# Attention, Mish MLP and gate on one core: eight inner tiles of the second product and the output projection are done by seven-product blocks in a tail, and five of sixteen probability tiles per head are summed by accumulating DMAs

## The chip, the cores and the metric

The kernel is one program on one core of a Trainium2 chip. The time is device time in microseconds (us) of one execution, the median over several. The engines are named as in the profile: PE is TensorE (matmuls; PEld is its weight load), DVE is VectorE, ACT is ScalarE, POOL is GpSimd, SP is SyncE, which here only issues DMAs. Each engine runs its own instructions strictly in the order in which they stand, and waits on semaphores for the others.

## The reference, cut to what matters

```
xn = layernorm(x)                                   # x: 2048 tokens x 1024
q, k, v = split(xn @ wqkv)                          # 32 heads of 32
p = softmax(q @ k.T * 32**-0.5)                     # per head 2048 x 2048
s = (p @ v) @ wo                                    # 1024 -> 1024
h = xn @ w1 + b1                                    # 1024 -> 3584
act = h * tanh(softplus(h))                         # Mish
out = x + s * silu(act @ w2)                        # w2: 3584 -> 1024
```

Everything is float32. Most products are kept accurate by cutting each operand into a high and a low part, and by adding three matmuls (high-high, high-low, low-high).

## The kernel before, in words

The program has four stretches. First, layer norm, the transposed and split activations, and v. Second, q and k by a seven-product block scheme. Third, one long mixed stretch, from about 530 us to the end of the last head, in which five streams share PE: `t` (transposed scores of a key tile, 128 keys x 2048 queries, as four matmuls of 512 columns, L1007), `s` (the same scores the other way round, for the row maxima of the next head, L920), `h` (the first MLP product, 24 matmuls for a tile of 128 inner features x 512 tokens, L1213), `y` (the second MLP product, L1303) and `pv` (probabilities times v, L1054). Fourth, the output projection `op` (L1402), with the silu and the gate behind it (L1495, L1496).

The third stretch is laid out ahead of time: a planner (class `Plan`) with a cost for every operation walks through time and writes each engine's order. Of the operations of an engine that are ready at that moment it takes the one with the lowest key. Operations that belong to the end have the key `2 * total` and are taken when nothing else of that engine is ready. A string of digits (`LEAN`) leans the choice in each piece of 21 us. The order, once written, is fixed; a wait that is longer on the chip than in the plan holds up all that stands behind it on its engine.

Per head there are sixteen key tiles (kt 0 to 15). ACT makes the exponentials of a tile into one of seven buffers `p` (four instructions, L285). PE multiplies the tiles by v in groups of 6, 5 and 5. The sum over keys for the softmax comes from POOL: fifteen additions of 128x2048 tiles into `z` (L1036), in the order of the tiles. When `z` is complete, PE reduces it over partitions (`zp`, L1080); `zp` also ends the life of `z`, of which there is one buffer, so that the first addition of the next head waits for it. ACT and DVE turn `zp` into the reciprocal and scale the head's output (L1091 to L1097).

The MLP makes 4 x 28 tiles of Mish (28 tiles `f` of 128 inner features, 4 chunks of 512 tokens). Each goes through twelve or thirteen instructions of DVE and ACT, ending with the split into high and low (L288, L1269). `y` takes them two at a time: 24 matmuls for each tile, and a DVE addition into the accumulator `yacc` for each block of 128 tokens x 512 columns (L1325). While the last heads run, POOL and DVE split the rows of wo (L296).

## Time and profile before

| what | value |
|---|---|
| median of three runs | 3362.5 us (3362.36 to 3362.78) |
| span of the profiled execution, first to last instruction | 3358.0 us |
| what lies outside the span (median less span; the profile gives no other time of that execution) | 4.5 us |
| PE busy in the span | 3345.8 us |
| POOL, DVE, ACT busy | 2524.7, 2510.8, 2056.5 us |
| granted PE clock | 1.00 in every slice |

A line of the groups reads: source line, engine, operation, output <- inputs, shape, count | busy us, mean ns of one | idle us of the engine just before them, and what ended it. Matmuls overlap in the pipeline, so that the duration of one is longer than the distance to the next; the distance is read from long runs of them.

### The profile page before, as it was taken

What the parts mean: (1) busy time and instruction counts of PE and PEld (TensorE: products, weight loads), DVE (VectorE), ACT (ScalarE), POOL (GpSimd) and SP (SyncE); (2) the same over time, 40 slices, a digit from 0 to 9 for tenths busy, and PEclk for the clock granted to TensorE, in tenths of its full rate; (3) what the DMA queues carried; (4) which work ended last, traced back from release to release, by engine and by line L of the source; (5) the groups of instructions that cost most, each with busy time, mean ns of one, the idle gap of its engine ahead of it and who ended that gap; (6) DMA issues with size and microseconds to landing.
All of it is one profiled execution on the core that took longest, in us unless ns stands there. A gap on an engine that the chain in (4) does not pass through costs nothing.

```text
span 3358.0 us, 45795 instructions
## 1 busy us (share of the span) xinstructions
PE 3345.8 (100%) x16886; PEld 2458.4 (73%) x16886; DVE 2510.8 (75%) x3987; ACT 2056.5 (61%) x3313; POOL 2524.7 (75%) x750
## 2 busy tenths in 40 slices
PE   9999999999999999999999999999999999999999
PEld 7888887776777677776777677777677777767787
DVE  6665678877877778887888688888787888886542
ACT  5233436676766666666676666666667666667621
POOL 1323546999999887888888988888888898889800
PEclk9999999999999999999999999999999999999999
DMA  7865745454565643343335334333344433433482
GB/s 248 298 204 181 242 146 183 140 184 152 169 191 172 221 126 115 105 122 114 101 117 179 111 101 126 101 112 116 101 151 139 116 106 112 130 108 107 140 304 83
DMA packets 291460, 501.56 MB, mean 149 GB/s; under 512 B 88138, under 2 KB 151114, under 8 KB 269130
## 3 DMA queue, kind: packets, MB, share of 16 engines
q1 hardware_dynamic: 271524, 456.95, 43.8%
q10 hardware_dynamic: 19712, 41.69, 3.3%
q8 instruction: 133, 2.18, 0.3%
q14 instruction: 91, 0.75, 0.1%
HBM read 352.55 MB, written 144.97 MB: 148 GB/s over the span
## 4 chain that ended last, share of the span: by engine, by line
PE 96%; DMA 1%; DVE 1%; POOL 1%; issue 0%; ACT 0%; SPq 0%; ACTq 0%; POOLq 0%; DVEq 0%
PE y L1303 18%; PE h L1213 18%; PE t L1007 14%; PE s L920 13%; PE pv L1054 13%; PE op L1402 5%; PE v L354 5%; PE q_y L798 3%; PE q_z L798 2%; PE q_x L798 2%; PE zp L1080 1%; PE s L700 0%; POOL z L1036 0%; PE pt L423 0%; DMA w2r<-in_B_w_dram 0%
## 5 line engine op out<-in xcount | busy, mean ns | idle before, releaser
L1036 POOL TENSOR_TENSOR z<-z,p 128x2048 f32<-128x2048 f32 x448 | 2067.7, 4615 | 98.0 <-ACT p L285 72.9
L285 ACT ACTIVATE p<-t,zero 128x512 f32<-128x512 f32 x2048 | 1377.1, 690 | 560.1 <-PE t L1007 535.7
L926 DVE TENSOR_REDUCE mx<-s 128x1 f32<-128x512 f32 x1984 | 1322.3, 685 | 382.7 <-PE s L920 371.9
L1303 PE MATMUL y<-w,act 128*128 128x512 f32 x2688 | 920.3, 391 | 0.8 <-DVE yacc L1325 0.5
L1007 PE MATMUL t<-qstack,kstack 128*128 128x512 f32 x2048 | 799.1, 393 | 1.1 <-ACT p L285 0.7
L920 PE MATMUL s<-kstack,qstack 128*128 128x512 f32 x1984 | 772.6, 393 | 0.2 <-ACT p L285 0.2
L1213 PE MATMUL h<-xr,w 128*128 128x512 f32 x2016 | 697.7, 391 | 0.4 <-DMA xr<-xs 0.4
L1303 PEld LDWEIGHTS y<-w,act 128*128 128x128 f32 x2688 | 503.3, 188 | 114.3 <-issue 6.7
L1007 PEld LDWEIGHTS t<-qstack,kstack 128*128 128x128 f32 x2048 | 383.8, 188 | 114.8 <-issue 18.0
L1054 PE MATMUL pv<-p,v 128*32 128x512 f32 x4096 | 459.3, 594 | 0.0
L920 PEld LDWEIGHTS s<-kstack,qstack 128*128 128x128 f32 x1984 | 369.6, 188 | 118.5 <-issue 32.1
L1213 PEld LDWEIGHTS h<-xr,w 128*128 128x128 f32 x2016 | 378.3, 188 | 81.2 <-issue 3.4
L1325 DVE TENSOR_TENSOR yacc<-yacc,y 128x512 f32<-128x512 f32 x416 | 282.7, 680 | 82.6 <-PE y L1303 81.5
L1054 PEld LDWEIGHTS pv<-p,v 128*32 128x32 f32 x4096 | 123.3, 110 | 282.7 <-issue 281.1
L1036 POOL TENSOR_TENSOR z<-p,p 128x2048 f32<-128x2048 f32 x32 | 148.1, 4628 | 185.2 <-PE zp L1080 146.6
L1213 PE MATMUL h<-xc,w 128*128 128x512 f32 x672 | 231.3, 391 | 1.3 <-DMA w<-w1s 1.0
L354 PE MATMUL v<-vw,xc 128*128 128x512 f32 x768 | 179.7, 392 | 1.2 <-ACT xc L288 0.7
L354 PEld LDWEIGHTS v<-vw,xc 128*128 128x128 f32 x768 | 142.7, 188 | 32.0 <-ACT xc L288 1.4
L1213 PEld LDWEIGHTS h<-xc,w 128*128 128x128 f32 x672 | 125.9, 188 | 30.5 <-issue 2.5
L288 ACT ACTIVATE act<-h 128x512 fp32r<-128x512 f32 x112 | 66.6, 595 | 88.2 <-DVE h L1262 87.0
L798 PE MATMUL q_y<-xc,wq 128*128 128x512 f32 x480 | 115.3, 389 | 0.0
L798 PEld LDWEIGHTS q_y<-xc,wq 128*128 128x128 f32 x480 | 90.0, 188 | 18.8
(149 smaller groups left out, 2947.4 us busy)
## 6 DMA issues: line engine op xcount, KB each, us to landing
w<-w1s SPq DMA_DIRECT2D x91, 1024.0 KB, 5.4
w<-w2s SPq DMA_DIRECT2D x168, 512.0 KB, 4.0
w2s<-w SPq DMA_DIRECT2D x56, 512.0 KB, 4.0
qstack<-qs SPq DMA_DIRECT2D x96, 256.0 KB, 6.3
kstack<-ks SPq DMA_DIRECT2D x96, 256.0 KB, 5.8
w1s<-w SPq DMA_DIRECT2D x21, 1024.0 KB, 5.8
qs<-qst ACTq DMA_DIRECT2D x32, 512.0 KB, 4.1
ks<-qst ACTq DMA_DIRECT2D x32, 512.0 KB, 3.7
```

The lines of the kernel that those rows point to most:

```text
L285: nc.scalar.activation(out_, in_, fn, bias=zero if bias is None else bias, scale=scale)
L354: nc.tensor.matmul(ps, xc[t // 4][k // HK][:, a, k % HK, (t % 4) * P:(t % 4 + 1) * P], vw[i, k // 2][:, b, k % 2], start=n == 0, stop=n == ...
L798: nc.tensor.matmul(ps, w[:, a, k], xx[:, b, k], start=m == 0 and i in (0, 1, 4), stop=m == 3 * HK - 1, skip_group_check=i not in (0, 1, 4))
L920: nc.tensor.matmul(sp_, qst[h % 3][:, qt * P:(qt + 1) * P], kst[h % 3][:, kc * 512:(kc + 1) * 512], start=True, stop=True)
L926: nc.vector.reduce_max(tiles["mx"][:, qt, kc:kc + 1], tiles[qt, kc], axis=AX.X)
L1007: nc.tensor.matmul(tp, kst[h % 3][:, kt * P:(kt + 1) * P], qst[h % 3][:, c * 512:(c + 1) * 512], start=True, stop=True)
L1036: nc.gpsimd.tensor_tensor(zs[h], pts[T - 1] if kt == 1 else zs[h], pts[T], ALU.add)
L1054: nc.tensor.matmul(pv[h][c * DH:(c + 1) * DH, :], vt[h][:, k, :], pts[T - kt + k][:, c * 512:(c + 1) * 512], start=k == 0, stop=k == NT - 1)
L1213: nc.tensor.matmul(t["h"], w1t[n][:, a, k], xts_[c][k // HK][:, b, k % HK], start=i == 0, stop=i == 3 * KT - 1)
L1303: nc.tensor.matmul(t["y"], acts[n][:, p, s * P:(s + 1) * P], w2t[m_][:, q], start=j == 0 and i == 0, stop=j == YB - 1 and i == 2)
L1325: nc.vector.tensor_tensor(ya, ya, t["y"], ALU.add)
L1402: nc.tensor.matmul(ps[t, dh], ohl[t // 4, k][:, a, s * P:(s + 1) * P], wt[k][:, b, r], start=k == 0 and i == 0, stop=k == KT - 1 and i == 2)
```

## The change

Three things are changed together.

**Deferral.** Of the 28 inner tiles, eight (f = 2, 5, 8, 11, 16, 19, 22, 25) take no part in `y` any more. Their Mish result (`r`, 128 features x 512 tokens, float32) goes to DRAM (`ats`), unsplit. The remaining twenty are taken in ten pairs.

**Tail.** The deferred part is a product of 2048 tokens x 1024 features by 1024 x 1024, the same size as the output projection. Both are done behind the last head as sixteen jobs of 256 tokens: jobs 0 to 7 with the deferred rows of w2 (set `y`), jobs 8 to 15 with wo (set `o`). A job cuts its operands into 2 x 2 blocks (128 tokens x 512 features, and 512 x 512) and forms the four block products from seven products of sums of blocks. Each product is 12 matmuls (4 pieces of 128 x 3 for high and low). The sums of the weight blocks (T1 to T4, in place) and their splits are made once for each set, the sums of the activations (S1 to S4) and their splits for each job. Jobs of set `y` add `ys`, go through silu and are stored (`gs`); jobs of set `o` load that and x and make the output. In the order's rows `yb`, `ob` are the weight blocks of the sets, `yu`, `ou` their split units 0 to 6, `araw` a job's activations, `a3_5` unit 5 of job 3, `op3_x` one of its three accumulators in PSUM, `e3_0` an evacuated copy, `g3` its gate rows.

**Sums in DRAM.** Tiles kt 0, 1, 6, 7 and 11 of each head are no longer added by POOL. kt 0 is written to DRAM (`zd`) by SP; the other four are added there by accumulating DMAs, which POOL issues. Each waits for the one before. After kt 11 SP reads the sum back into a `p` buffer (`zp19` and the like in the order, not to be confused with the PE reduction `zp`), and POOL merges it into `z`. POOL's chain is then ten additions and the merge, where it was fifteen additions; the additions of kt 12 to 15 stand behind the merge.

In the last part of the diff `mm7` is the 12 matmuls of a product, `a_unit` and `b_unit` are a split (ACT the high part, DVE the low part), `after` takes the accumulators out of PSUM, `done` finishes a block, job 7 is `NP - 1`, and `LAG` is three products.

Three constants of the planner go with it (`SLOW`, `Y1`, and 0.5 instead of 4.0 us for `zp` in `LATE_Z`); `LEAN` stays as it was.

```diff
-    SEM, SWITCH, LAND, RATE = 0.07, (0.25, 0.13), 2.0, 0.25e6
+    SEM, SWITCH, LAND, RATE, SUM = 0.07, (0.25, 0.13), 2.0, 0.25e6, 7.0
...
-SLOW, UNTIL = 1.25, 700.0
+SLOW, UNTIL = 1.1, 700.0
+DEFER = (2, 5, 8, 11, 16, 19, 22, 25)
+KEPT = [f for f in range(FT) if f not in DEFER]
+BLOCKS = [KEPT[i:i + 2] for i in range(0, len(KEPT), 2)]
-LEAD, LATE = 5, 4.0
-PS, ACTS, W2S, Y0, Y1 = 7, 3, 5, 0.6, 0.17
+THERE = (0, 1, 6, 7, 11)
+HERE = [kt for kt in range(NT) if kt not in THERE]
+LEAD, LATE, LATE_Z = 5, 4.0, 0.5
+PS, ACTS, W2S, Y0, Y1 = 7, 3, 5, 0.6, 0.25
...
-            op.end = start + took
+            op.end = start + took + (self.SUM if op.bytes else 0.0)
...
     def add(T, pts):
         h, kt = divmod(T, NT)
+        def there(at):
+            if kt:
+                nc.gpsimd.dma_start(zd[h % 2], pts[T], accum_op=ALU.add)
+            else:
+                nc.sync.dma_start(zd[h % 2], pts[T])
+        def back(at):
+            pts[h, "z"] = att.tile([P, S], F32, tag=f"p{at['p']}", name=f"zp{h}")
+            nc.sync.dma_start(pts[h, "z"], zd[h % 2])
+        def merge(at):
+            nc.gpsimd.tensor_tensor(zs[h], zs[h], pts[h, "z"], ALU.add)
...
+        if kt in THERE:
+            d = op("POOL" if kt else "SP", 1.2 if kt else 0.1, need=exps[T] + [dma.get(h)], emit=there, bytes_=P * S * 4,
+                   then=then, key=-1)
+            dma[h] = d
+            if kt == THERE[-1]:
+                dma[h] = op("SP", 0.1, need=[d], emit=back, take=["p"], bytes_=P * S * 4)
+                chain[h] = op("POOL", 4.61, need=[chain[h], dma[h]], emit=merge, give=[("p", dma[h])])
...
-        a = own = op("PE", 1.0, need=[sum_], emit=z_mm, take=["d", "b"], give=["z"], col=True, late=LATE)
+        a = own = op("PE", 1.0, need=[sum_], emit=z_mm, take=["d", "b"], give=["z"], col=True, late=LATE_Z)
...
+        if n % FT in DEFER:
+            o6 = op("DVE", 0.69, need=[o5, o3], emit=d6_, give=[("d", t["own"]), ("b", t["own"]), "h"], kind="mish")
+            put_ops[n] = op("SP", 0.1, need=[o6], emit=put, give=["r"], bytes_=P * 512 * 4)
+            return
...
+    def tail_stream():
+        far = 2 * total
+        def sum_(which, need):
+            return op("POOL", 4.61, need=need, emit=lambda at: b_sum("y", which, nc.gpsimd), key=far)
+        def split(i, need, take):
+            h_ = op("ACT", 1.9, need=need, emit=lambda at: b_high("y", i), take=take)
+            return op("POOL", 4.61, need=[h_], emit=lambda at: b_low("y", i, nc.gpsimd), key=far)
...
+    for j in range(last + 1):
+        for i in range(7):
+            mm7(j, i)
+            nxt = j + 1
+            if j == 0:
+                if i < 6:
+                    a_unit(0, i + 1)
+                if i == 0:
+                    b_low("y", 3, nc.vector)
+                if 0 < i < 4:
+                    b_unit("y", i + 3)
+            later.tick()
+            after(j, i)
+            if j == NP - 1:
+                if i == 3:
+                    b_sum("o", "T4", nc.gpsimd)
+                if i == 4:
+                    b_sum("o", "T1", nc.gpsimd)
+                b_unit("o", i)
+                if i == 0:
+                    b_sum("o", "T2", nc.vector)
+            if nxt <= last:
+                if i == 1:
+                    for which in ("S1", "S2", "S3"):
+                        a_sum(nxt, which, nc.gpsimd, small(f"{nxt}{which}", which))
+                later.at(LAG, lambda nxt=nxt, i=i: a_unit(nxt, i))
+            if i == 1:
+                out_load(j)
+            if i >= 4:
+                for n in {4: (4,), 5: (2, 5), 6: (6,)}[i]:
+                    done(j, n)
```

How the order moves, at three places.

POOL, one head in the middle. Before, fifteen additions in a row (rows of head 17, the middle ones left out):

```order
L1036 TENSOR_TENSOR z17_18797<-p272_18688,p273_18720 128x2048
L1036 TENSOR_TENSOR z17_18797<-z17_18797,p274_18793 128x2048
...
L1036 TENSOR_TENSOR z17_18797<-z17_18797,p286_19358 128x2048
L1036 TENSOR_TENSOR z17_18797<-z17_18797,p287_19404 128x2048
L1036 TENSOR_TENSOR z18_19590<-p288_19451,p289_19488 128x2048
```

Now (head 19, kt 6 is tile p310, kt 11 is p315; `hl` is a 0.2 us subtraction for the next head's maxima):

```order
L1044 DMA zd1_161<-p310_19657 128x2048
L1055 TENSOR_TENSOR z19_19579<-z19_19579,p312_19746 128x2048
L1044 DMA zd1_161<-p311_19707 128x2048
L1055 TENSOR_TENSOR z19_19579<-z19_19579,p313_19783 128x2048
L306 TENSOR_TENSOR hl_3351<-nm20_0_19863,hl_3351 128x16
L1055 TENSOR_TENSOR z19_19579<-z19_19579,p314_19812 128x2048
L1044 DMA zd1_161<-p315_19846 128x2048
L1058 TENSOR_TENSOR z19_19579<-z19_19579,zp19_20031 128x2048
L1055 TENSOR_TENSOR z19_19579<-z19_19579,p316_19925 128x2048
```

The DMA issues stand in POOL's queue between the additions, and the merge stands right behind the last issue, with nothing of POOL's between them.

POOL, the last head. Before, nothing stood between its additions (first, second and last, then the tile of wo that followed):

```order
L1036 TENSOR_TENSOR z31_29501<-p496_29370,p497_29394 128x2048
L1036 TENSOR_TENSOR z31_29501<-z31_29501,p498_29499 128x2048
...
L1036 TENSOR_TENSOR z31_29501<-z31_29501,p511_29984 128x2048
L296 TENSOR_TENSOR wo4_30066<-wr2_30007,wo4_30066 128x1024
```

Now, from its ninth tile on:

```order
L306 TENSOR_TENSOR yu0_0_28693<-yb0_27551,yu0_0_28693 128x2048
L1055 TENSOR_TENSOR z31_28541<-z31_28541,p505_28627 128x2048
L1044 DMA zd1_161<-p507_28752 128x2048
L1055 TENSOR_TENSOR z31_28541<-z31_28541,p506_28672 128x2048
L1399 TENSOR_TENSOR yb0_27551<-yb1_27553,yb0_27551 128x2048
L306 TENSOR_TENSOR yu2l_28708<-yb2_28255,yu2h_28707 128x2048
L1058 TENSOR_TENSOR z31_28541<-z31_28541,zp31_28881 128x2048
L306 TENSOR_TENSOR yu1_1_28917<-yb0_27551,yu1_1_28917 128x2048
L1055 TENSOR_TENSOR z31_28541<-z31_28541,p508_28789 128x2048
L1399 TENSOR_TENSOR yb2_28255<-yb2_28255,yb0_27551 128x2048
L1055 TENSOR_TENSOR z31_28541<-z31_28541,p509_28813 128x2048
...
L1055 TENSOR_TENSOR z31_28541<-z31_28541,p511_28867 128x2048
```

Five passes of the tail's set-up (three splits, two weight sums) stand inside the last head's chain. On PE the reduction of that chain, `zp31`, stands ahead of the tail's first product.

ACT, where the tail goes from set `y` to set `o`. This stretch has no counterpart before.

```order
L298 ACTIVATE ou4_30091<-ob0_29212 128x2048
L298 ACTIVATE a8_2_30107<-araw8_29908 128x512
L298 ACTIVATE ou5_30111<-ob2_29484 128x2048
L295 ACTIVATE g7_30022<-g7_30022,zero_174 128x1024
L298 ACTIVATE a8_3_30130<-araw8_29908 128x512
L298 ACTIVATE ou6_30133<-ob3_29620 128x2048
L295 ACTIVATE g7_30022<-g7_30022,zero_174 128x1024
L298 ACTIVATE a8_4_30152<-8S1_30017 128x512
L298 ACTIVATE e8_0_30155<-op8_x_30139 128x512
```

The copy `e8_0` that frees job 8's first accumulator for its third product stands behind the last units of set `o` and behind both silu instructions of job 7.

More of the change, by code (lines that the diff above doesn't have):

```diff
@@ L990, in p_done @@
         if len(uses[T]) == 2:
-            plan.give("p", max(o.end for o in uses[T]))
+            plan.give("p", max(o.end for o in uses[T]), by=exps[T][0])
     def t_stream():
@@ L1357, in wo_raw @@
-    def wo_raw(name, ks, tile_of, **kw):
-        a = raw_op(name, 2, tile_of, [(("wo", k), wo[k * P:(k + 1) * P, :], []) for k in ks], **kw)
-        for k, o in zip(ks, a):
-            wo_loads[k] = o
-    def wo_op(k, where, eng, **kw):
-        def high(at):
-            wt[k] = where()
-            copy(wt[k][:, 0], raws_["wo", k])
-        def rest(at):
-            low(nc.gpsimd if eng == "POOL" else nc.vector, wt[k][:, 1], raws_["wo", k], wt[k][:, 0])
-        need = kw.pop("need", [])
-        a = op("ACT", 1.05, need=[wo_loads[k]] + need, emit=high, **kw)
-        wo_ops[k] = op(eng, 2.36 if eng == "POOL" else 1.3, need=[a], emit=rest, key=2 * total if eng == "POOL" else None,
-                       both=eng == "DVE")
@@ new lines, in b_low, with a_load @@
+    def b_low(set_, i, eng):
+        low(eng, units[set_, i][1], weights[set_, SOURCE[i]], units[set_, i][0])
+    jobs = [(set_, p) for set_ in "yo" for p in range(NP)]
+    def a_load(j, tile_):
+        set_, p = jobs[j]
+        araw[j] = tile_.rearrange("p (k n) -> p k n", k=KT)
+        if set_ == "y":
+            nc.sync.dma_start(araw[j], ats[p // 2][:, p % 2])
+            return
+        for k in range(KT):
+            nc.sync.dma_start(araw[j][:, k], ot[k][:, p * 256:p * 256 + 256])
@@ new lines, in mm7 @@
+    def mm7(j, i):
+        set_ = jobs[j][0]
+        if i in (0, 1, 4):
+            n = bank_sets[j % 2][KEYS[i]]
+            banks_[j, KEYS[i]] = bank({"b": n}, f"op{j}_{KEYS[i]}")
+        ps = banks_[j, KEYS[i]]
+        m = 0
+        for k in range(HK):
+            for a, b in THREE:
+                nc.tensor.matmul(ps, units[j, i][:, a, k], units[set_, i][b][:, k], start=m == 0 and i in (0, 1, 4),
+                                 stop=m == 3 * HK - 1, skip_group_check=i not in (0, 1, 4))
+                m += 1
@@ new lines, in tt, with after @@
+    def tt(eng, out_, a, b, how):
+        eng.tensor_tensor(out_, a, b, how)
+    def after(j, i):
+        set_, p = jobs[j]
+        ps = banks_[j, KEYS[i]]
+        if i in (0, 1, 3):
+            es[j, i] = tl.tile([P, 512], F32, tag=f"e{i}", name=f"e{j}_{i}", bufs=1 if i == 3 else 2)
+        V, G = nc.vector, nc.gpsimd
+        if i == 0:
+            copy(es[j, 0], ps)
+        elif i in (1, 3):
+            tt(V, es[j, i], ps, es[j, 0], ALU.add)
+        elif i == 4:
+            tt(V, es[j, 3], ps, es[j, 3], ALU.add)
```

356 lines of the change are left out of this document (191 added, 165 removed).

## The prediction

> **What bounds the kernel now.** First the page's head and the busy shares, then the table by stage (us from the start, then busy time and instructions of PE, PEld, DVE, ACT, POOL), then who PE waited for.
>
> ```profile
> span 3358.0 us, 45795 instructions
> PE 3345.8 (100%) x16886; PEld 2458.4 (73%) x16886; DVE 2510.8 (75%) x3987; ACT 2056.5 (61%) x3313; POOL 2524.7 (75%) x750
> PEclk9999999999999999999999999999999999999999
> 700.00:1000.00 300.00, 298.64 (x1535) 214.20 (x1534) 236.73 (x376) 210.85 (x345) 283.46 (x107) 1.00 0.54 170
> 2200.00:2600.00 400.00, 399.59 (x2089) 282.11 (x2088) 319.69 (x509) 273.12 (x434) 348.24 (x82) 1.00 0.41 123
> PE idle L473 <- POOL xc L470: 1.8, 1, 1.8
> PE h L1213 <- DMA w<-w1s: 1.0, 1, 1.0
> ```
>
> PE sets the time in every stage, at full clock, and its longest single wait is 1.8 us, at the start. POOL is next: 94% early, where it also splits weights, 87% later. So a matmul removed is time gained, as long as no wait takes its place. Before, no wait of note exists; the question is how many the new order makes. I sum from the profiled execution: span 3358.0 plus the 4.5 outside it, which is the median, 3362.5.
>
> **Matmuls removed.** By the order `y` falls from 2688 to 1920 and `op` rises from 768 to 2 x 672 = 1344: 192 fewer. Their distance comes from the longest piece of the chain (start, length, what):
>
> ```profile
> 3179.26 174.11 PE op L1402 x768
> ```
>
> 174.11/768 = 0.2267 us, and 192 of them are **-43.5**.
>
> PE leaves the pv/zp form and comes back 114 times where it did 97 times, since zp now goes as soon as it is ready. The price, from one visit (start, length, what):
>
> ```profile
> 2162.66 0.62 PE L1303 MATMUL y<-w,act 128*128 128x512 f32 x2
> 2163.21 5.36 PE L1054 MATMUL pv<-p,v 128*32 128x512 f32 x48
> 2168.50 0.50 PE L920 MATMUL s<-kstack,qstack 128*128 128x512 f32 x1
> 2168.84 0.40 PE L1007 MATMUL t<-qstack,kstack 128*128 128x512 f32 x1
> ```
>
> In: 0.55 - 2 x 0.2267 = 0.10; out: 0.34 - 0.23 = 0.11. 17 visits are **+4**. The same rows give 5.29/6 = 0.88 us for one key tile of pv. The yacc additions and splits that go with `y` lie on DVE and ACT beside PE: nothing.
>
> **POOL against PE, head by head.** The loop that can stall is: zp of a head frees `z`; POOL then does the whole chain of the next head, with everything that stands between; then PE may do that head's zp.
>
> ```profile
> L1036 POOL TENSOR_TENSOR z<-z,p 128x2048 f32<-128x2048 f32 x448 | 2067.7, 4615 | 98.0 <-ACT p L285 72.9
> L1036 POOL TENSOR_TENSOR z<-p,p 128x2048 f32<-128x2048 f32 x32 | 148.1, 4628 | 185.2 <-PE zp L1080 146.6
> L296 POOL TENSOR_TENSOR w<-w2r,w 128x512 fp32r<-128x512 f32 x56 | 72.5, 1295 | 32.6 <-ACT w L288 32.6
> 3100.40 4.62 POOL L1036 TENSOR_TENSOR z<-p,p 128x2048 f32<-128x2048 f32 x1 [5.54 <-PE zp L1080]
> 3105.10 66.82 POOL L1036 TENSOR_TENSOR z<-z,p 128x2048 f32<-128x2048 f32 x14
> ```
>
> Before, POOL waits for zp, not PE for POOL. Counting by the order tests this: from the last-but-one zp to the last, PE has 271 matmuls and 16 tiles of pv (61.4 + 14.1 + about 0.7 = 76.2), POOL 15 additions at 66.82/14 = 4.77 or a little less (70 to 71.5): POOL idles about 5, and the row says 5.54.
>
> Now the same for the change, an addition at 4.67 (4.615 and the gap). Middle heads: ten additions, the merge, four DMA issues: 51.4 + 4 x 1.2 + 0.3 = 56.5 against 65 to 83 of PE. No DMA issue of POOL's stands in the trace. The lower bound is ACT's issue below, 0.34; the upper the addition that it replaces, 4.6; I take 1.2, nearer the issue, since POOL only hands the transfer on.
>
> - **Third head** (560 to 700 us): PE has 204 matmuls and 10 tiles of pv, 55.8. POOL has 51.4, eight splits at 1.3, issues: 67. **+12** (8 to 25). The fifth head, with the wait for DRAM below, adds about **+3**.
> - **Last head**: PE has 182 matmuls and 10 tiles, 50.5. POOL has the 51.4, two sums of weights (9.3), three splits of 128x2048 and three issues (3.6).
>
> ```profile
> L288 ACT ACTIVATE wo<-wr x8: 1042/1053/1062, 3013.1 to 3190.4; 128x1024 fp32r<-128x1024 f32 x8
> L296 POOL TENSOR_TENSOR wo<-wr,wo x4: 2386/2410/2827, 3016.6 to 3181.0; 128x1024 fp32r<-128x1024 f32 x4
> L296 DVE TENSOR_TENSOR wo<-wr,wo x4: 1212/1225/1662, 3160.7 to 3191.5; 128x1024 fp32r<-128x1024 f32 x4
> ```
>
> A split of 128x2048 is thus 4.8 on POOL: three are 14.5, and POOL's total is 78.8. PE stands at zp31 for **+28** (25 to 38), with y and pv all done and the tail queued behind it.
>
> **The sums in DRAM.** After the kt 11 exponentials come the issue, the accumulation A, the read-back B, the merge and four additions, then zp.
>
> ```profile
> w<-w1s SPq DMA_DIRECT2D x91, 1024.0 KB, 5.4
> w1s<-w SPq DMA_DIRECT2D x21, 1024.0 KB, 5.8
> xr<-xs SPq DMA_DIRECT2D x12, 1024.0 KB, 7.8
> 3333.09 0.34 ACTq L1500 DMA_DIRECT2D out_dram<-x  x1
> DMA packets 291460, 501.56 MB, mean 149 GB/s; under 512 B 88138, under 2 KB 151114, under 8 KB 269130
> ```
>
> B is 5.4 to 7.8. A is not in the trace: at least a plain write, 5.8, at most read and write in turn, 11.2; I take 7.5, nearer the write, since a stream can overlap both. A + B = 13.3. By the order PE has 40.6 of work between the end of kt 11's scores and zp in the tightest middle heads. Off go 0.9 for the exponential and the hops, 1.2 for the issue, and 24.6 for the merge, four additions and the next head's first issue; 14.0 is left for A + B, and 16 in the median head: **0**. At A + B = 19 (the upper ends) the shortfalls over the heads add up to 77. POOL itself stands still during A + B, but has that slack. The `p` buffers don't tie up more: the five tiles wait for their pv group anyway.
>
> **The tail.** A job is 84 matmuls, 19.0; a product 2.72. In an ordinary job DVE has about 10 to 12 and POOL 10 to 14: covered. Two jobs are not, because their weight splits are made as they go, through chains that cross three engines. Further rows:
>
> ```profile
> L296 DVE TENSOR_TENSOR wq<-raw,wq 128x512 fp32r<-128x512 f32 x20 | 15.5, 778 | 6.5 <-ACT wq L288 6.4
> L1496 DVE TENSOR_TENSOR x<-x,y 128x512 f32<-128x512 f32 x32 | 22.1, 692 | 1.1
> L288 ACT ACTIVATE wq<-raw 128x512 fp32r<-128x512 f32 x29 | 17.9, 623 | 30.1 <-PE q_x L798 13.8 <-PE q_z L798 10.5 <-issue 3.9
> L285 ACT ACTIVATE rz<-rz,zero 128x512 f32<-128x512 f32 x32 | 23.5, 733 | 0.3
> L1094 DVE SCALAR_TENSOR_TENSOR zp<-zp,rz 128x512 f32<-128x512 f32 x32 | 22.1, 692 | 0.1
> L285 ACT ACTIVATE y<-y,zero 128x1024 f32<-128x1024 f32 x16 | 18.3, 1142 | 31.3 <-DVE x L1496 31.2
> ```
>
> From the wo rows a 128x2048 high is about 1.9 on ACT, and a low 2.4 to 3.3 on DVE; I take 2.6.
>
> - **Job 0** (us from zp). DVE's normalisation of the last head stands ahead of S1 and S2. So product 1 waits for two activations and three DVE steps (4.0 with the hops), S1 and S2 (6.0), a high and a low (7.5). Product 0 covers 2.7 of it: 4.8 lost. Product 2 waits for unit 3's low and a small split (11.2, PE free at 10.2). Product 3 waits for POOL's T1 (11.0), unit 4's high and low (15.6), the sum `e` and a split (17.0, PE free at 13.9). Two more lows cost 0.5 and 1.9 in the same way. **+11** (6 to 16).
> - **Jobs 7 and 8** (us from the start of job 7). Product 0 ends at 2.7. Then come the copy `e` (3.5), unit 0's high and low (8.1), T2 on DVE (10.9), unit 1's high and low (15.6), a small split and unit 2's low (18.9). On POOL T4 and T1 follow (28.1), on ACT and DVE unit 4 (32.8). From here the rows of ACT's order shown above run one behind the other, with DVE between: a split (33.5), unit 5's low (36.1), two gate sums (37.5), silu (38.7), a high and unit 6 (44.0), a gate sum and silu (45.9), a high and the copy `e8_0` (47). Job 8's third product adds into the accumulator that this copy reads, and PE was free for it at 26. **+22** (12 to 30).
> - **Jobs 8 to 15.** SP loads a job's gate rows and x behind the store that waits for the previous job's last gate; the loop (load about 10, five POOL steps, DVE) is as long as the job. **+3** (0 to 15).
>
> **The clock.** PE starts cold once in the trace:
>
> ```profile
> 1.82 4.63 PE L473 MATMUL idle<-xc 128*128 128x512 f32 x10 [1.82 <-POOL xc L470]
> ```
>
> Ten matmuls take 4.63 where 2.27 is due: 2.4 lost. No later stop is long enough to show whether that comes back. Four long stops: between 0 and 9.4; I take **+6**, as the one start from rest is the nearest row.
>
> The Trainium skill (TensorE: Matmul & The Clock Gate, Part 1) says that the clock halves after an idle window of about 3.4 us and is back after 3.4 us of work. By it each stop would cost an estimated 1.7 us, four of them 7; this speaks against any change that opens such gaps, and no run so far shows it.
>
> **Sum:** -43.5 + 4 + 15 + 28 + 0 + 11 + 22 + 3 + 6 = +45. 3358.0 + 4.5 + 45 = **3408 us**, slower.
>
> **Rivals.**
>
> *Loads, not chains, decide the tail (faster).* If each engine's work per job counts, and the cross-engine chains hide behind the three products of lag, jobs 0 and 8 lose nothing, nor does the clock, and the third head's wait drains into its neighbours' slack: -43.5 + 4 + 28 = -11, **3351**. For it: by the same count POOL has 12 and 19 us of slack in the heads before and after the third, and DVE is busy about 60% of an ordinary job. Against it: a queue in order cannot lend slack forward past a wait. It decides where the chains and the early wait together stay under 5 us.
>
> *Half of it (no change).* The chains cost about half (16), the clock nothing, the early wait 3: -43.5 + 4 + 28 + 16 + 3 = +8, **3370**; just above what I call no change.
>
> *DRAM sums are slow (much slower).* With A + B = 19 the room is short in most heads: 3408 + 77 = **3485**; with an issue that holds POOL for 4.6, more. For it: the DMA engines are already busy 41 to 54% (last column but one of the stages), and per head six more tiles of 1 MB move, 192 MB beside the page's 501.56. Against it: 5.4 to 5.8 for plain transfers of that size under the same load. It decides from A + B = 14.
>
> That the change does not do what it says is excluded by the order: 192 matmuls and 128 additions are gone.
>
> **Chances.** Forecast 0.63 (its own range 3374 to 3440), chains hidden 0.11, half 0.10, slow sums 0.16. 0.2% (6.7 us) is what a measurement of this kernel can tell from no change: faster 0.11, same 0.08 (the half case and the edge of the first), slower 0.81. The low bounds of the terms give -43.5 + 4 + 8 + 25 + 6 + 12 = +11, 3374; the range reaches a little below, into the half case, and up to the slow sums: 3364 to 3485.
>
> **What would show it.** Right: PE's waits name POOL `z` once with over 25 us, near the last head; a stop of about 20 in the tail that follows an ACT copy `e`; and zp waits of some 12 in the third head. The granted clock dips behind them. Wrong: zp waits spread over all heads (DRAM sums slow), a PE that is busy throughout the tail (first rival), or DMA issues on POOL that last several us. The forecast as a whole falls if the stops add up to less than 37.

## The result, and the profile after

| | before | after |
|---|---|---|
| median of four runs, us | 3362.4 (3362.4 to 3362.8) | 3513.9 (3512.3 to 3515.9) |
| span of the profiled execution, us | 3358.0 | 3513.3 |
| mean granted PE clock | 1.000 | 0.983 |

The ratio is 1.0449 (95% 1.0434 to 1.0464). The change costs 151 us; 45 were forecast. The sign was right, and the time lies above the upper end of the range, 3485.

The head of the page after, its transfers as a whole, and the queue on which POOL issues the accumulating transfers (packets, MB, share of the 16 engines' time):

```profile
span 3513.3 us, 46019 instructions
PE 3378.5 (96%) x16694; PEld 2435.8 (69%) x16694; DVE 2605.7 (74%) x3973; ACT 2093.6 (60%) x3367; POOL 2264.2 (64%) x874
DMA packets 317958, 702.91 MB, mean 200 GB/s; under 512 B 91082, under 2 KB 170442, under 8 KB 266954
q0 software_dynamic: 18432, 134.23, 20.6%
```

Fewer matmuls keep PE busy longer, 3378.5 us for 3345.8: part of the loss is idle time, part is a slower PE. The stages show where. The columns are those of the table by stage in the prediction; the last three are granted clock, DMA share and GB/s.

```profile
700.00:1000.00 300.00, 282.52 (x1343) 190.37 (x1342) 212.71 (x341) 195.85 (x324) 231.21 (x93) 0.95 0.74 204
2200.00:2600.00 400.00, 397.21 (x2079) 273.82 (x2081) 318.82 (x504) 275.82 (x440) 272.54 (x81) 1.00 0.76 206
3100.00:3150.00 50.00, 23.27 (x110) 13.71 (x108) 30.13 (x15) 9.07 (x11) 43.42 (x11) 0.73 0.30 111
3300.00:3350.00 50.00, 27.92 (x92) 21.57 (x91) 41.41 (x25) 19.95 (x21) 27.30 (x11) 0.76 0.22 77
```

The last two rows are the places that the prediction named, the last `zp` and the turn from job 7 to job 8. The first row is not: between 700 and 1000 us, where PE lost 1.4 us before, it now loses 17.5, and the clock is at 0.95. In the middle (second row) POOL went from 348 busy us to 273 and the DMA share from 0.41 to 0.76, and PE lost little. The waits of PE over the whole span (in total, times, longest):

```profile
PE zp L1110 <- POOL z L1055: 29.8, 4, 25.3
PE t L1017 <- ACT p L295: 16.9, 14, 4.1
PE op_y L1552 <- DVE e L1557: 16.7, 9, 6.6
PE op_x L1552 <- ACT e L298: 11.0, 3, 7.0
PE s L930 <- ACT p L295: 9.8, 5, 3.8
```

**A count by stage.** Waits alone miss short hitches and the clock. So I set the time between two `zp` against the work that PE has there by the order: 0.2267 us for a matmul, 0.89 for a key tile of pv, 0.21 for a visit to the pv/zp form. In after the 7th `zp` starts at 1199.4 us, the 31st at 3060.8, and the 32nd is this row:

```profile
3137.92 1.93 PE L1110 MATMUL zp<-z,ones 128*32 128x512 f32 x8 [25.30 <-POOL z L1055]
```

What is over and above that work, in us of the profiled executions:

| | work | to the 7th zp | 7th to 31st | last head | behind the last zp |
|---|---|---|---|---|---|
| before | 3322.1 | 21.6 | 9.4 | 0.0 | 4.9 |
| after | 3282.1 | 104.5 | 31.5 | 25.5 | 69.7 |
| difference | -40.0 | +83 | +22 | +25.5 | +65 |
| forecast | -39.5 | +15 | 0 | +28 | +36 |

The forecast had 6 more for the clock, which in the count lies inside the stages. Up to the 7th `zp`, while the weights of the MLP are split, 68 us more went than was forecast; behind the last `zp` 29 more, in the middle 22.

**The early stage.** In these heads the raw halves of w1 and w2 are loaded, cut by ACT (high) and POOL (low), and stored. A piece of the chain of waits of after (start, length, what):

```profile
1083.08 1.31 POOL w L306
...
1084.82 11.38 DMA w1r<-in_B_w_dram
...
1097.46 1.17 ACT p L295 x2
...
1098.67 0.50 PE t L1017
```

POOL ends one half; only then can the next be loaded into the same place; it takes 11.38 us to land; ACT stands in front of it; behind the activation for this half, in ACT's fixed order, are the exponentials; PE waits for them. ACT's waits for raw weights between 550 and 1200 us, before (line L288) and after (L298):

```profile
ACT w L288 <- DMA w2r<-in_B_w_dram: 9.1, 6, 2.7
ACT w L288 <- DMA w1r<-in_B_w_dram: 1.7, 1, 1.7
```

```profile
ACT w L298 <- DMA w1r<-in_B_w_dram: 42.8, 18, 4.6
ACT w L298 <- DMA w2r<-in_B_w_dram: 24.1, 15, 6.3
```

From 10.8 us to 66.9. Before, no half of w1 took more than 6.1 us to land (row in experiment 6). So the first theory: the transfers of the DRAM sums make the weight loads late, and PE waits behind ACT. Its rivals: the deferral did it (less PE work over the same splits, and SP's stores of the deferred results); the accumulation did it, not the traffic; the denser early plan did it (`SLOW` 1.1).

### The profile page after: what moved, and what is told of

The parts are those of the page before. It is cut to its first block, busy times and chain, and to the rows that moved or that the text cites. A ratio compares the mean times of both kernels' runs of the same rounds, so it can differ in the third digit from the quotient of the medians.

```text
span 3513.3 us, 46019 instructions
## 1 busy us (share of the span) xinstructions
PE 3378.5 (96%) x16694; PEld 2435.8 (69%) x16694; DVE 2605.7 (74%) x3973; ACT 2093.6 (60%) x3367; POOL 2264.2 (64%) x874
## 3 DMA queue, kind: packets, MB, share of 16 engines
q0 software_dynamic: 18432, 134.23, 20.6%
## 4 chain that ended last, share of the span: by engine, by line
PE 54%; POOL 8%; DMA 6%; DVE 3%; issue 3%; ACT 2%; SPq 0%; POOLq 0%; DVEq 0%; ACTq 0%
PE h L1243 13%; PE t L1017 10%; PE pv L1087 10%; PE s L930 10%; PE y L1343 8%; POOL z L1055 3%; DMA w1r<-in_B_w_dram 2%; DMA zd<-p 1%; PE op_y L1552 1%; PE op_z L1552 1%; ACT p L295 1%; PE zp L1110 1%; DVE a L306 1%; POOL g L1557 1%; DMA zp<-zd 1%
## 5 line engine op out<-in xcount | busy, mean ns | idle before, releaser
L1055 POOL TENSOR_TENSOR z<-z,p 128x2048 f32<-128x2048 f32 x288 | 1351.4, 4692 | 60.3 <-ACT p L295 47.5
L1017 PE MATMUL t<-qstack,kstack 128*128 128x512 f32 x2048 | 804.5, 399 | 22.3 <-ACT p L295 16.9
L1243 PE MATMUL h<-xr,w 128*128 128x512 f32 x2016 | 709.7, 391 | 1.2 <-DMA xr<-xs 0.8
L1343 PE MATMUL y<-w,act 128*128 128x512 f32 x1920 | 689.8, 393 | 9.0 <-ACT p L295 7.6
L1343 PEld LDWEIGHTS y<-w,act 128*128 128x128 f32 x1920 | 360.6, 188 | 93.9 <-ACT p L295 8.9
L1058 POOL TENSOR_TENSOR z<-z,zp 128x2048 f32<-128x2048 f32 x32 | 147.3, 4604 | 342.7 <-DMA zp<-zd 272.6
L1365 DVE TENSOR_TENSOR yacc<-yacc,y 128x512 f32<-128x512 f32 x288 | 195.8, 680 | 59.4 <-PE y L1343 58.7
L1243 PE MATMUL h<-xc,w 128*128 128x512 f32 x672 | 217.0, 411 | 1.7 <-DMA w<-w1s 1.3
L1044 POOL DMA_DIRECT2D zd<-p x128 | 113.3, 885 | 87.1 <-ACT p L295 60.4
L306 DVE TENSOR_TENSOR a<-araw,a 128x512 fp32r<-128x512 f32 x80 | 109.2, 1378 | 16.1 <-ACT a L298 16.1
```

What stands on the lines that cost most here:

```text
L306: eng.tensor_tensor(out_, in_, high.bitcast(F32), ALU.subtract)
L1017: nc.tensor.matmul(tp, kst[h % 3][:, kt * P:(kt + 1) * P], qst[h % 3][:, c * 512:(c + 1) * 512], start=True, stop=True)
L1055: nc.gpsimd.tensor_tensor(zs[h], pts[h * NT + HERE[0]] if kt == HERE[1] else zs[h], pts[T], ALU.add)
L1058: nc.gpsimd.tensor_tensor(zs[h], zs[h], pts[h, "z"], ALU.add)
L1243: nc.tensor.matmul(t["h"], w1t[n][:, a, k], xts_[c][k // HK][:, b, k % HK], start=i == 0, stop=i == 3 * KT - 1)
L1343: nc.tensor.matmul(t["y"], acts[n][:, p, s * P:(s + 1) * P], w2t[m_][:, q], start=j == 0 and i == 0, stop=j == YB - 1 and i == 2)
```

## The experiments

All times are medians of four runs, and ratios are to the kernel before on the same chip. "Early" is the loss to the 7th `zp` by the count above.

**1. All sums back on POOL.**

```
+FROM = 99                      # THERE is empty for heads below FROM
+    THERE, HERE = there_of(h), here_of(h)
```

> All 15 additions of every head back on POOL, no sums in DRAM; deferral, tail and constants as in the changed kernel. Theory (the transfers of the DRAM sums make the raw weight loads late while the weights are split, ACT stands in front of each late weight and PE behind ACT): the 89 us lost up to 1200 us fall to the roughly 22 us by which POOL's longer chain is short of PE's work in heads 2 to 6, the 19 us of the middle heads go, and the last head (22 short by count) and the tail stay: 3514 - 67 - 19 = about 3428 us, 3410 to 3445; ACT's waits for w1r and w2r fall from 67 us to about 10 as before the change. Rival (the deferral itself: less PE work over the same splits, and SP's stores of the deferred results that wait for DVE): the early loss stays and POOL's shortage comes on top, 3490 us or more.

Measured: 3451.3 us, ratio 1.0266 (1.0251 to 1.0282). Early 48.6, middle 23.3, last head 24.2, tail 71.3. The time is 6 us above the expected range, and ACT's waits for raw weights are 22.3 us, where about 10 were expected. So 56 of the 83 us that the early stage lost go with the DRAM sums. The middle gains 8 where 19 were expected, and 27 early stay with the deferral. POOL's shortage by the order is 22 there, nearly all of it in one head (16.3), which loses 17.1.

**2. The sums alone, in the kernel before.** Its `add` is replaced by the changed one, with `THERE`, `SUM` and `LATE_Z`; nothing is deferred.

> The kernel before with only the sums in DRAM (same five tiles, read-back and merge, zp free to come as a visit of its own): no deferral, no new tail, the early slow-down of the plan at 1.25. Theory (transfers make weight loads late): 40 to 90 us lost between 550 and 1200 us, 3405 to 3455 us, with ACT's waits for raw weights above 40 us and PE's waits naming ACT p there. Rival (the deferral did it): only the extra visits of the zp form, about 29 at 0.21 us, 3369 us, and ACT's waits for raw weights near 11 us.

Measured: 3468.6 us, 1.0308 (1.0286 to 1.0329): above the expected range. Early 91.7, middle 30.6, last head 6.9, tail 10.5. The DRAM sums cost 106 us by themselves, though by the order POOL is ahead of PE in every head. Nor did POOL's standing for the sums do it: between 550 and 1200 us it stood at the merges for 8.6 us. ACT's waits for raw weights are 70.4 us in the same stretch. The rival (deferral) falls as the main cause.

**3. Plain writes in place of accumulations.** This kernel leaves out what the four transfers of a head should add; a second line, not shown, adds 1 under the logarithm.

```
-nc.gpsimd.dma_start(zd[h % 2], pts[T], accum_op=ALU.add)
+nc.gpsimd.dma_start(zd[h % 2], pts[T])
```

> The four accumulating transfers of a head are plain writes of the same tile to the same place from the same queue (what they should add is left out, and the logarithm of the denominators takes 1 more so that it stays finite); same instructions, waits and order. If the accumulation itself is slow (read and write in turn), its landing falls from 8.9 us to 6 or less and most of the early loss of 89 us and of the middle's 19 goes: about 3430 us. If it is the mere traffic and the queueing of six more tiles per head, little changes: 3490 to 3514 us.

Measured: 3457.3 us, 1.0285 (1.0270 to 1.0301). Early 59.9, middle 18.2. The time lies between the two that were expected, 57 us under after. The transfer itself, of after and then of this kernel (ns min/median/max of the issue on POOL; us to landing; at last, from its page, the queue's share of the 16 engines, which was 20.6% in after):

```profile
L1044 POOL DMA_DIRECT2D zd<-p x128: 805/880/1202, 537.6 to 3091.1; - x128
...
DMA to landing us min/median/max: 7.6/8.9/14.7
```

```profile
L1044 POOL DMA_DIRECT2D zd<-p x128: 531/571/723, 537.1 to 3032.7; - x128
...
DMA to landing us min/median/max: 4.2/4.9/11.2
```

```profile
q0 software_dynamic: 18432, 134.23, 9.7%
```

The same bytes, order and waits; the accumulation takes 20.6% x 3513.3 / 128 = 5.7 us of all sixteen engines for a tile, the write 9.7% x 3456.0 / 128 = 2.6. That is worth 45 of the early loss and 13 of the middle. SP's order is the same in both, so it is not what made the loads late. What differs is the engines' time, and 0.31 us of POOL for an issue, which is under 9 us over the 28 issues of seven heads. The Trainium skill (DMA: Bandwidth & Descriptors, Issuing engines are not separate DMA queues) says that transfers from any issuing engine run on the same sixteen DMA engines and interleave there. These two runs agree: what POOL issues delays what SP issues.

**4. The early plan slow again.** `SLOW` 1.25 for 1.1.

> Only the plan's early slow-down back at 1.25 from 1.1, so that the heads of the first 700 us are spread wider over the weight splits. If the late weight loads alone set the early loss (DMA engines too busy whatever the order), it stays: 3505 to 3520 us. If the denser early plan is half of it, the early 89 us fall to about 45 and the time to about 3470 us.

Measured: 3527.0 us, 1.0488 (1.0470 to 1.0505). Early 107.8, and the time is 7 us above the range given for no effect. A denser early plan is not the cause.

**5. The sums from head 7 on.** `FROM = 7` in the first experiment's code.

> Sums in DRAM only from head 7 on, when no weight is split any more; heads 0 to 6 add all on POOL. Theory (the DRAM sums hurt by colliding with the weight loads; in the middle they cost little and the pool slack they buy is worth little): the stages add up, early 49 us lost as with all sums on POOL, middle 31 and last head 25 as in the changed kernel, tail 70: 3283 + 175 = 3458 us, 3445 to 3470. Rival (the accumulations hurt wherever they run, by what they do to DMA and POOL): the middle is no better than with all sums on POOL and heads 7 to 12 carry the loss on, 3490 us or more.

Measured: 3469.6 us, 1.0317 (1.0303 to 1.0333). Early 46.5, middle 41.0 (7.9 in head 7), last head 28.6. The stages add up, apart from 9.5 us more in the middle. Without weights to split, 24 heads of DRAM sums cost 18 us against all sums on POOL; with them, the first seven cost 56.

**6. A later landing in the plan.**

```
-SEM, SWITCH, LAND, RATE, SUM = 0.07, (0.25, 0.13), 2.0, 0.25e6, 7.0
+SEM, SWITCH, LAND, RATE, SUM = 0.07, (0.25, 0.13), 5.0, 0.25e6, 7.0
```

> The changed kernel with one constant of the plan: a load is taken to land 5.0 us after its issue in place of 2.0 (plus bytes over rate), so that the plan puts ACT's split of a raw weight behind more exponentials. Theory (loads land later than the plan has them, ACT's queue in order then holds the exponentials PE waits for): the loss up to the seventh zp, 104 us by the count of work against time, falls to about 55 to 65, PE's waits for ACT p between 550 and 1200 us fall from 29 us to under 10: about 3470 us. Rival (the serial loop of load, split and store of 82 weight halves is itself the bound there, each turn longer): the place of the splits doesn't matter, 3505 us or more.

Measured: 3528.7 us, 1.0494 (1.0477 to 1.0512): the rival's outcome. PE's waits for ACT p between 550 and 1200 us fell as the theory said, from 29 us to 4.5, and the loss stayed: early 91.6, middle 56.3. It changed its form. PE of this kernel (start, length, what, idle time before):

```profile
1233.44 0.51 PE L930 MATMUL s<-kstack,qstack 128*128 128x512 f32 x1 [0.56 <-DVE mx L936]
1233.79 0.40 PE L1017 MATMUL t<-qstack,kstack 128*128 128x512 f32 x1
1234.70 0.50 PE L930 MATMUL s<-kstack,qstack 128*128 128x512 f32 x1 [0.51 <-DVE mx L936]
```

Here only `s` and `t` are left to PE, a pair in 1.2 us, as fast as DVE's maxima and ACT's exponentials let them; PE could do a pair in 0.45. Few `h` matmuls stand between them: 38 from 1200 to 1250 us, where after has 66, while the last halves of w1 are still being split. That they wait for these weights is the likely reason. The splits of w1 on POOL, first to last start, of before, after and this kernel, with the time from issue to landing of their loads where the trace gives it:

```profile
L296 POOL TENSOR_TENSOR w<-w1r,w x42: 1277/1294/1332, 645.9 to 1088.8; 128x512 fp32r<-128x512 f32 x42
...
DMA to landing us min/median/max: 3.1/4.8/6.1
```

```profile
L306 POOL TENSOR_TENSOR w<-w1r,w x42: 1262/1284/1613, 661.5 to 1180.7; 128x512 fp32r<-128x512 f32 x42
```

```profile
L306 POOL TENSOR_TENSOR w<-w1r,w x42: 1264/1286/1587, 653.7 to 1249.4; 128x512 fp32r<-128x512 f32 x42
...
DMA to landing us min/median/max: 2.9/6.5/7.6
```

443, 519 and 596 us for the same 42 halves. So the first theory was half of it at most. The second: each half goes through one place (load, ACT, POOL, next load), and that loop sets the pace of `h`. A turn took 10.8 us before and 14.5 here (443 and 596 over 41 turns), of which the median landing is 4.8 and 6.5. A longer landing lengthens each turn, and moving ACT's part behind the landing lengthens it once more.

**7. Two places for the raw halves.** They need room, which one of the five weight tiles of `y` gives. The place of w1's halves (`on`) also holds each head's output, which thus gets a second place too. So first the control with four tiles, then the two places, then these with the later landing in the plan.

```
-PS, ACTS, W2S, Y0, Y1 = 7, 3, 5, 0.6, 0.25
+PS, ACTS, W2S, Y0, Y1 = 7, 3, 4, 0.6, 0.25     # control
-("on", 1)  ("w2r", 1)
+("on", 2)  ("w2r", 2)                          # and the tiles' tags by their place
-b = op("SP", 0.1, need=[a] + need, emit=raw, ...)
+b = op("SP", 0.1, need=[b] + need, emit=raw, ...)
```

> The changed kernel with four instead of five tiles for the weights of the second product: the control for the next kernel, which needs their room. By every theory the weights of y come a little later: 3510 to 3535 us.

> As the control, and two places instead of one for the raw halves of w1 and for those of w2, so that a load flies while the half before it is split. New theory (the loss up to the seventh zp comes from the serial loop of load, ACT, POOL, next load, each turn as long as a load's landing, which the accumulations lengthen; PE is short of h and does s and t instead, faster than ACT and DVE can follow): with loads overlapped the loss of 104 us falls by at least 40 against the control: 3470 us or less. Rival (the DMA engines, at 70 to 90% there, are the bound whatever is in flight): within 15 us of the control.

> As the one with two places each, and the plan takes a load to land 5.0 us after its issue. With the loop no longer the bound, the place of ACT's splits should matter: stops over 1 us go, and the time is another 10 to 30 us under that kernel's, 3440 to 3465 us. If the loop is still the bound: no difference or slower, as it was without the second places.

| | us | ratio | early | middle | early + middle |
|---|---|---|---|---|---|
| control | 3533.5 | 1.0511 (1.0495 to 1.0526) | 88.5 | 59.4 | 148 |
| two places | 3487.1 | 1.0371 (1.0356 to 1.0387) | 73.1 | 33.8 | 107 |
| and landing 5.0 | 3464.6 | 1.0304 (1.0287 to 1.0322) | 34.9 | 43.6 | 79 |

Two places gain 46 us against the control, and the time stayed 17 above the expected bound. Only 15 of the 46 are early. Some 24 fall in the 24th to 31st head and 5 in the last, long after the last raw half (1194 us in the control); what made these heads better is not shown. The control alone, with one tile less and the order that the planner made of it, lost 16 less early than after and 28 more in the middle, so 15 us in one stage decide nothing. The third kernel does: early it loses 34.9 where the control lost 88.5. With the loop opened, the place of ACT's splits counts as first thought, where by itself it had made things worse. The rival (the engines are the bound whatever is in flight) falls with it: between 550 and 1200 us their busy share rose from 0.77 in the control to 0.85 while the loss fell. The 42 splits then take 439 us, as before the change:

```profile
L306 POOL TENSOR_TENSOR w<-w1r,w x42: 1273/1299/1817, 650.7 to 1089.8; 128x512 fp32r<-128x512 f32 x42
```

**8. The same two cures without the deferral, and without the DRAM sums.** The first is experiment 2 with the edits of 7. The second is experiment 1 with them, and with the last head's weight sums and splits on DVE (experiment 9).

> The kernel before with the sums in DRAM alone, and the two cures of the weight stage: two places for the raw halves (and four tiles for the second product's weights in place of five), and 5.0 us for a landing in the plan. Theory (the DRAM sums cost what they do because each half weight goes through one place and ACT's place in the order was planned for an earlier landing): of the 92 us lost up to the seventh zp without the cures 35 to 45 are left, as in the changed kernel, 3410 to 3430 us. Rival (in the full kernel the cures helped by something that the deferral brought): 3450 us or more.

> The deferral and its tail without sums in DRAM, with both cures of the weight stage and the last head's weight sums and splits on DVE. Theory (the deferral's own early loss, 49 us against 22 in the kernel before, is the same loop of raw weights, with less of PE's work over it): early loss 25 to 32, middle 20, last head 3 to 8, tail 70, work 3280: 3400 to 3410 us. Rival (it is something else, POOL's additions or ACT's and DVE's share of the stage): early loss 45 or more as with 1.25 in the plan, 3420 us or more.

Measured: 3398.4 us, 1.0105 (1.0090 to 1.0120), and 3415.6 us, 1.0155 (1.0139 to 1.0172). Early 33.4 for 91.7, and 29.3 for 48.6. The first is 12 us better than its range. The second is 6 us over: its last head still loses 13.6, and the tail 71.5.

For the DRAM sums this shows the loop. With the same transfers, 58 of their 70 early us are gone; ACT's waits for raw weights fall from 70.4 us to 10.7, POOL is not short by count in either kernel, and the engines' share from 550 to 1200 us rises from 0.76 to 0.85. For the deferral it does not. The sixth head, in which POOL was short by 16.3 in experiment 1, lost 17.1 there; in the new order POOL is not short in it, and it loses 4. How much of the deferral's 27 early us is the loop, with less of PE's work beside the same loads, and how much POOL's shortage, stays open.

One run stands between, made when POOL's shortage was the only theory for the deferral's early loss: no DRAM sums, `SLOW` back at 1.25, the last head's sums and splits on DVE.

> No sums in DRAM (all 15 additions of a head on POOL), the early slow-down of the plan back at 1.25, the tail's weight sums and splits of the last head on DVE: what the deferral and its tail cost once the other losses are cured as far as the runs showed how. By count POOL is short by 22 us in heads 2 to 6 and 3 in the last. Work 3284, early loss 40 to 45, middle 20, last head 3 to 5, tail 70: 3415 to 3430 us. Rival (the early loss of the deferral is not POOL's shortage): 3451 less 20 for the last head at most, 3432 us or more.

Measured: 3442.2 us, 1.0238 (1.0223 to 1.0253), with 54.1 lost early: the rival's side. POOL's shortage, 22 by count in this kernel too, was not all of its loss.

**9. The last head.** The two weight sums and three splits of the tail go to DVE.

```
-return op("POOL", 4.61, need=need, emit=lambda at: b_sum("y", which, nc.gpsimd), key=far)
+return op("DVE", 2.4, need=need, emit=lambda at: b_sum("y", which, nc.vector), key=far, both=True)
-return op("POOL", 4.61, need=[h_], emit=lambda at: b_low("y", i, nc.gpsimd), key=far)
+return op("DVE", 2.6, need=[h_], emit=lambda at: b_low("y", i, nc.vector), key=far, both=True)
```

> Only the two sums and three splits of the tail's weights that stand among the last head's additions on POOL go to DVE. Theory (POOL's chain of the last head, 78.0 us by count against 50.7 of PE): the chain becomes 54.1, the stop before the last zp falls from 25.3 us to about 3 to 6 and the cold restart after it shortens: 3514 - 20 to 23 = 3491 to 3494 us. Rival (DVE, which shares the work of that stage, becomes late for the first job, or is slowed beside POOL): the loss moves into job 0, 3505 us or more.

Measured: 3512.5 us, 1.0447 (1.0431 to 1.0462): no difference that can be told from after. In the profiled execution the stop fell from 25.3 to 14.8 us. POOL of this kernel, last head:

```profile
3091.52 0.89 POOL L1044 DMA_DIRECT2D zd<-p  x1
3105.77 6.36 POOL L1058 TENSOR_TENSOR z<-z,zp 128x2048 f32<-128x2048 f32 x1 [13.37 <-DMA zp<-zd]
```

With the splits gone, POOL stands for the sum in DRAM: 13.4 us from the end of the issue to the merge. In after the splits had filled this gap. By count the chain is 54.1 + 13.4 against 50.7 of PE: 17 short, and the last head lost 18.3. The expectation had left A + B, the time of the sum in DRAM and its read-back, out because before it was hidden by the very work that was moved.

**10. e ahead of the splits in the tail.** `after(j, i)` and `later.tick()` swapped.

> In the tail the step that folds a product into e (ACT copy or DVE addition) is put ahead of the next job's splits in the queues, two lines swapped. Theory (in each of the jobs 8 to 15 PE waits 1.2 us because two splits of 2.86 us together stand ahead of the addition e on DVE, slowed beside POOL): 7 x 1.35 = 9 us gone, jobs 7 and 8 little changed: 3504 us. Rival (the loop of gate rows, x and POOL's gates sets the o jobs' length): the wait only moves, 3511 to 3516 us.

Measured: 3517.5 us, 1.0463 (1.0448 to 1.0479): the rival. A job of set `o` starts 20.4 us after the one before, where it was 20.55. PE's waits for ACT's `e` are named 8 times in the tail, where they were 3; the wait moved. What sets the length of these jobs this run does not show.

## Why the prediction was wrong

**Matmuls and visits (-43.5 and +4): right.** PE's work by the order fell by 40.0.

**The sums in DRAM (0): the step that failed.** Its arithmetic held. A + B was set at 13.3; the last head of experiment 9 shows 13.4, though A alone is 8.9 for the 7.5 taken. The issue on POOL was set at 1.2 and takes 0.88. POOL stood at the merge for the sum in 23 heads, 273 us in all, as the step said:

```profile
POOL z L1058 <- DMA zp<-zd: 272.6, 23, 28.1
```

PE hardly noticed: its waits for `zp` are 4.5 us outside the last head. The step asked only who waits for the sum. It did not ask who else uses the sixteen DMA engines. Accumulations take 5.7 us of all of them for a tile, and the loads of raw weights, which had landed in 4.8 us and go through a single place each, became late. The slow-sums rival had the traffic in view (192 MB, which is 201 in the unit of the page's 501.56, and engines 41 to 54% busy) and came within 29 us of the time, but by another mechanism, and so by luck: it expects `zp` waits spread over all heads, and outside the last head three are named, 4.5 us in all. In the kernel before, this mechanism alone costs 70 us early (91.7 less 21.6). In the middle the sums cost 21 more there; why was not looked into, beyond the 13 that plain writes took from after.

**Third and fifth head (+15): hidden, neither shown nor refuted.** No `zp` wait is named before 1200 us, so the sign that was given did not come. But POOL's count of 67 against 55.8 stands in the order, and in the third head POOL's last addition ended at 799.6 us, only 1.2 before `zp` (5.5 in the kernel before). PE was held up in the same heads by the weights, so that the two losses lie over each other, and no run parts them. Without the DRAM sums the deferral cost 27 early, with POOL short by 22.

**Last head (+28): right,** 25.3 for the stop and 25.5 by count, for the reason given; under it lay a second bound of 17, the DRAM sum.

**The tail (+11, +22, +3): places right, most sizes small, the chain between jobs 7 and 8 right only in part.** Matmuls of after at the stops and behind them:

```profile
3307.65 4.77 PE L1552 MATMUL op_y<-yu,a 128*128 128x512 f32 x12 [6.60 <-DVE e L1557]
3326.39 5.46 PE L1552 MATMUL op_z<-yu,a 128*128 128x512 f32 x12 [8.51 <-DVE e L1557]
3344.35 0.80 PE L1552 MATMUL op_x<-ou2h,a 128*128 128x512 f32 x1 [6.96 <-ACT e L298]
```

Against 19.04 for 84 matmuls, job 0 took 12.5 more, jobs 7 and 8 together 29.9, jobs 9 to 15 10.9, jobs 1 to 6 6.9. The gate behind the last matmul takes 9.1 us where the old output took 4.6. The first two hold 4.0 and 6.7 for the clock; without it they are 8.5 and 23.2, against 11 and 22. But the one stop of about 20 behind the copy `e8_0` came as three: the first two rows stand in job 7, behind additions `e` of DVE, and only the third, 6.96, is that copy. That the sum fits is luck in part. Jobs 1 to 6 were put at nothing, and the small repeated losses were mis-sized: a split of 128x512 on DVE was priced at 0.778 from the rows of before. Whether that sets the length of these jobs, no run shows.

```profile
L306 DVE TENSOR_TENSOR a<-araw,a 128x512 fp32r<-128x512 f32 x79 | 90.8, 1163 | 16.1 <-ACT a L298 16.1
L1557 DVE TENSOR_TENSOR e<-op_y,e 128x512 f32<-128x512 f32 x32 | 21.9, 685 | 8.9 <-PE op_y L1552 8.9
```

In the tail (3130 to 3513 us) it takes 1.16 on the mean, while an addition of the same size with one input in PSUM stays at 0.685. The Trainium skill (SBUF — State Buffer, Who interferes with whom) says that a DVE instruction with two SBUF inputs shares a read path with GpSimd, and one with a single SBUF input does not. These rows agree.

**The clock (+6): too few stops.** See below; five restarts from the last `zp` on cost 10.7, and early the clock fell to 0.95 of full over 300 us, which is 14 us of 282.5 busy.

Of the signs that the prediction listed, the stop before the last `zp` and the dips of the clock came; the stop of about 20 came in pieces, and the `zp` waits in the third head did not come. It listed `zp` waits over all heads as the sign of slow sums; the sign was ACT's wait for weights.

No kernel here beats the one before. With the early loop and the last head cured, the deferral still loses what its tail costs, 65 us more than the old output, against 40 of work saved. Making the units of the second set ahead, against the 30 us of jobs 7 and 8, was not tried.

## What to carry to other kernels

Ask of an added transfer not only who waits for it but whose loads share the engines, and look first for loops with a single buffer: load, split, next load. Each turn contains a whole landing, and whoever stands in order behind the late step pays. A price for an accumulating transfer cannot be taken from a plain write of the same size. And a stop is the largest of several bounds: before moving the work that fills it, work out the next one. Where a planner lays the order anew for each variant, losses also move between stages (16 and 28 us in the control of experiment 7), so that a difference of that size in one stage shows little.

## What the runs showed of the hardware

- An accumulating DMA of 1 MB into DRAM took 8.9 us to land and 0.88 us to issue on POOL; a plain write from the same queue 4.9 and 0.57. In engine time the ratio is 2.2.
- PE stops of some 2 us and more can cost more than their length. The same stop in the tail, in after and then in the kernel of experiment 9:

```profile
3179.27 0.50 PE L1552 MATMUL op_x<-yu2h,a 128*128 128x512 f32 x1 [2.33 <-ACT e L298]
3179.60 0.40 PE L1552 MATMUL op_x<-yu2l,a 128*128 128x512 f32 x1
3179.84 0.63 PE L1552 MATMUL op_x<-yu2h,a 128*128 128x512 f32 x2
3180.31 0.39 PE L1552 MATMUL op_x<-yu2l,a 128*128 128x512 f32 x1
```

```profile
3172.30 0.50 PE L1552 MATMUL op_x<-yu2h,a 128*128 128x512 f32 x1 [2.32 <-ACT e L298]
3172.64 0.44 PE L1552 MATMUL op_x<-yu2l,a 128*128 128x512 f32 x1
3172.88 1.06 PE L1552 MATMUL op_x<-yu2h,a 128*128 128x512 f32 x2
3173.74 0.63 PE L1552 MATMUL op_x<-yu2l,a 128*128 128x512 f32 x1
```

In the first, matmuls start 0.24 apart from the second on, and the granted clock stays at 1.00. In the second, they start 0.43 apart from the third on, and the clock is at 0.56 over 3 us. So the length of a stop of 2.3 us does not decide it. Over the kernels of this case, the change and its experiments, the clock was halved after each of 114 stops of 3.0 us or more, and after 17 of the 28 between 2.0 and 2.5 us that had no other stop close by. The stops of 4.2 to 25 us at the last `zp` and in the tail of after were followed by 1.7 to 2.7 us lost each, whatever their length. The Trainium skill (TensorE: Matmul & The Clock Gate, Part 1) has the clock halved after an idle window of about 3.4 us; these traces show it after shorter stops too. For a schedule it means that many stops of 2 to 4 us, as behind late weights, can cost half as much again or more.
